# Grouped-query attention and a gated feed-forward: where q and k are transposed, and where the spatial bias is added

## The chip, the core and the metric

The kernel runs on one core of one Trainium2 chip. The metric is the device time of one execution in microseconds. TensorE (PE in the profile, with PEld for its weight loads) does matmuls, VectorE is DVE, ScalarE is ACT, GpSimd is POOL, and SyncE (SP) issues most of the DMAs. [...]

## The reference

Eight batches of attention, 16 query heads on 4 key heads, 384 positions, head size 64; its output, rows of 1024, goes through a feed-forward with a gate that mixes positions.

```python
scores = scale * np.matmul(q, k.transpose(0, 1, 3, 2))
scores = scores - np.max(scores, axis=-1, keepdims=True)
attn = np.exp(scores)
attn = attn / (np.sum(attn, axis=-1, keepdims=True) + 1e-09)
x = np.matmul(attn, v)                      # per head, then heads side by side
h = np.maximum(x @ w_in, 0.0)
u, v = (h[..., :d_ff // 2].copy(), h[..., d_ff // 2:].copy())
v_n = (v - mu) / np.sqrt(var + 1e-06)       # mu, var over the last axis
v_s = np.einsum('ts,bsd->btd', w_spatial, v_n) + b_spatial[None, :, None]
gated = u * v_s
return (gated @ w_out).astype(np.float32)
```

All inputs and the output are fp32; the matmuls take fp16. `w_spatial` is 384 x 384, `b_spatial` has 384 entries.

## The kernel before

A batch is worked in nine visits (`vi` 0 to 8, the loop at line 457). A visit issues two of the 18 score units of its batch (`scores`, L268: two matmuls of 512 columns into a two-bank PSUM tile `sc`, of which there are two; then one ScalarE exponential, L281, into `aT`). Four times a batch, at the visits of `VALUES_AT`, comes `values`: the sums of the exponentials (`sums`), their reciprocal on ScalarE (`rec`, a logarithm and an exponential), and two products with v (`X`), which VectorE multiplies by `rec` into `xT` (L312).

The feed-forward of batch b-1 runs between the visits of batch b, from a queue of 17 pieces: three `mk_v` (`pv`, relu on ScalarE, statistics and normalisation on VectorE into `v_n`), four `mk_u` (`pu`, relu on VectorE into `uT`, L371), four `mk_sp` (`psp`, the spatial product of one 128-wide slice m of the features, gated into `gT`, L389), six `mk_out` (`po`, L403, which contracts over all four slices of `gT`; VectorE copies it out, L410, and SP stores it). Each piece has a planned cost; per visit, pieces are taken until the spent cost passes a budget (`per_visit`, line 454). The last feed-forward runs alone at the end.

PE, POOL and SP follow the order in which the program issues their instructions; the order on VectorE and ScalarE is left to the scheduler. Eight PSUM banks are in use: four for the two score tiles, and four that all other products share in turn (the pool `ps`).

At visit 2 of batch b, `load_batch` (line 134) loads k, q and v of batch b+1 in fp32 and casts them to fp16: on POOL, but for k and the first half of q of batch 1, which VectorE casts. q and k have to be transposed before the scores. Batch 0 does so on PE (`transpose_k`, `transpose_q`: six 128 x 128 transposes into a PSUM tile `pk` or `pq`, then one VectorE copy of 768 fp16 a partition, L244 and L258). Batches 1 to 7 do so by DMA from SBUF to SBUF, issued on SP (`dma_transpose_k`, `dma_transpose_q`, L221 and L228): k and the first half of q (`gp` 0) at visit 6 of the batch before, the second half at visit 8.

The spatial bias is one number per output position, that is per column of `psp`. It is added by a first matmul (L380) of a matrix of ones rows with `bias_rows`, which holds the bias as two fp16 rows, a high and a low part. `load_bias` makes them once (L172 to L174), from a 1.5 KB load.

On POOL, the weights of the feed-forward are loaded in the opening by 34 DMAs with a cast from fp32 (L188, L194), in its queue ahead of the casts of v and of the second half of q of batch 1.

Of the kernel before, what the change touches and what calls it, by code (L numbers as in the profile page):

```python
# [10 lines left out]
FP32 = mybir.dt.float32  # L11
FP16 = mybir.dt.float16
# [6 lines left out]
def kernel(  # L19
# [92 lines left out]
    def cast_k(b, engine):  # L112
        k16 = qk16.tile([P, NGP, NST, 2, D], FP16, name=f"k16_{b}", tag="k16")
        k32 = loaded["k32", b].rearrange("p (gp h) (t d) -> p gp t h d", gp=NGP, t=NST)
        for gp in range(NGP):
            engine.tensor_copy(k16[:, gp], k32[:, gp])  # L116
        loaded["k16", b] = k16
# [6 lines left out]
    def cast_q(b, gp, engine):  # L124
        q16 = qk16.tile([P, G, NST, 2, D], FP16, name=f"q16_{b}_{gp}", tag=f"q16_{gp}")
        q32 = loaded["q32", b, gp]
        for half in range(2):
            engine.tensor_copy(
                q16[:, :, :, half, :],
                q32[:, half * G : (half + 1) * G, :].rearrange("p j (t d) -> p j t d", t=NST),  # L130
            )
# [17 lines left out]
    bias_rows = cst.tile([P, S], FP16, name="bias_rows")  # L149
    bias_ones = cst.tile([P, P], FP16, name="bias_ones")  # L150
# [4 lines left out]
    def load_consts():  # L155
# [4 lines left out]
        nc.vector.memset(bias_rows, 0.0)  # L160
        nc.vector.memset(bias_ones, 0.0)
        nc.vector.memset(bias_ones[0:1, :], 1.0)
        nc.vector.memset(bias_ones[32:33, :], 1.0)

    def load_bias():
        b32 = cst.tile([1, S], FP32, name="b32")
        lo32 = cst.tile([1, NST, P], FP32, name="lo32")
        nc.sync.dma_start(b32, moe_b_spatial.rearrange("(a s) -> a s", a=1))
        b_tp = b32.rearrange("a (p t) -> a t p", t=NST)
        hi = bias_rows[0:1, :].rearrange("a (t p) -> a t p", t=NST)  # L170
        lo = bias_rows[32:33, :].rearrange("a (t p) -> a t p", t=NST)
        nc.vector.tensor_copy(hi, b_tp)  # L172
        nc.vector.tensor_tensor(lo32, b_tp, hi, ALU.subtract)
        nc.vector.tensor_copy(lo, lo32)  # L174
# [44 lines left out]
    def dma_transpose_k(b):  # L219
        kT[b] = tr_sb.tile([P, NGP, NST, P], FP16, name=f"kT_{b}", tag="kT")  # L220
        nc.sync.dma_start_transpose(  # L221
            kT[b].rearrange("p g t q -> p (g t) q"),
            loaded["k16", b].rearrange("p g t h d -> p (g t h d)"),
        )

    def dma_transpose_q(b, gp):
# [295 lines left out]
```

## Time and profile before

| | us |
|---|---|
| median of 3 runs (lowest to highest) | 290.18 (289.11 to 290.86) |
| the profiled execution | 289.11 |
| its span, first to last instruction | 287.3 |
| start of pv_0, batches 0 to 7 of the feed-forward | 41.1, 74.6, 106.7, 138.6, 170.4, 202.9, 235.3, 264.1 |

Each step of the last row but the first and the last is one batch. The profile by stretches of about one batch, with the busy time of each engine and the mean granted clock of PE:

```profile
75.00:107.00 32.00, 30.44 (x278) 13.34 (x276) 16.61 (x31) 22.73 (x32) 4.92 (x7) 1.00 0.65 153
107.00:139.00 32.00, 30.58 (x278) 13.46 (x277) 16.14 (x31) 23.03 (x33) 4.93 (x7) 1.00 0.66 156
...
235.00:267.00 32.00, 31.80 (x280) 14.45 (x280) 16.58 (x32) 19.59 (x28) 0.00 (x0) 1.00 0.16 65
```

The columns are the stretch, its length, the busy time and instruction count of PE, PEld, DVE, ACT and POOL, the clock, the mean busy share of the DMA engines and the GB/s. A matmul's duration in the profile reaches past the start of the next one[...]; the distance between two starts is what a matmul costs. An idle stretch of an engine is shown in square brackets behind the instruction that ended it, with what released it.

### The profile page before, as it was taken

Reading aid. Unit: us, or ns where it says so; the run is one execution under the profiler, and the core shown is the slowest. Engines: PE = TensorE matmul, PEld = TensorE weight load, DVE = VectorE, ACT = ScalarE, POOL = GpSimd, SP = SyncE. Lnnn points to the kernel's source line nnn. Section 1 sums busy time; section 2 is a strip of 40 time slices with the busy share of each in tenths; the row PEclk is TensorE's granted clock in tenths of the full one; section 3 lists DMA queues with packets and bytes.
Section 4 is the critical chain, followed back from the end, with each engine's and each line's share of the span. In section 5 each row is a group of like instructions: output and inputs, shape, how many; then the busy total and the mean of one; then the engine's idle time right before and its main releaser. Section 6 shows DMA issues by size and latency. Waiting matters only on the chain.

```text
span 287.3 us, 5420 instructions
## 1 busy us (share of the span) xinstructions
PE 255.2 (89%) x2247; PEld 113.3 (39%) x2247; DVE 143.8 (50%) x277; ACT 184.4 (64%) x249; POOL 54.0 (19%) x88
## 2 busy tenths in 40 slices
PE   0685879989899989999899989999899989999993
PEld 0431234444344334444344434443344434444551
DVE  3427116474365443574365434674365434575673
ACT  1485895757676686758676776658676786664300
POOL 0654870600140004200150003300150000000000
PEclk9998599999999999999999999999999999999998
DMA  7999999906691479709790549406790530003105
GB/s 215 331 252 124 147 142 216 287 20 198 203 260 29 112 157 312 108 0 203 227 248 13 130 160 329 70 2 202 241 245 2 128 148 0 2 29 121 73 0 219
DMA packets 59402, 42.42 MB, mean 148 GB/s; under 512 B 29041, under 2 KB 55666, under 8 KB 59378
## 3 DMA queue, kind: packets, MB, share of 16 engines
q1 hardware_dynamic: 56274, 38.94, 53.6%
q0 software_dynamic: 3104, 3.15, 7.9%
q8 instruction: 17, 0.28, 0.4%
q14 instruction: 7, 0.06, 0.1%
HBM read 25.76 MB, written 12.58 MB: 133 GB/s over the span
## 4 chain that ended last, share of the span: by engine, by line
PE 75%; ACT 11%; DMA 6%; DVE 4%; issue 1%; SPq 1%; POOL 0%
DMA ws_318<-in_moe_w_spatial_dram 4%; DMA q_0_1_136<-in_q_dram 3%; ACT aT_1_337 L281 1%; ACT aT_0_2652 L281 1%; ACT aT_0_2216 L281 1%; ACT aT_0_471 L281 1%; ACT aT_0_1780 L281 1%; ACT aT_0_1344 L281 1%; ACT aT_0_3088 L281 1%; ACT aT_0_908 L281 1%; ACT aT_1_3288 L281 1%; ACT aT_1_686 L281 1%; SPq L106 1%; DVE ws_320 L204 1%; PE pv_0_3166 L327 1%
## 5 line engine op out<-in xcount | busy, mean ns | idle before, releaser
L364 PEld LDWEIGHTS <-w_in_107 128*128 128x128 f16 x256 | 23.4, 98 | 22.8 <-issue 8.8
L188 POOL DMA_DIRECT2D w_in_107<-in_moe_w_in_dram x32 | 17.2, 544 | 8.1 <-DMA w_in_107<-in_moe_w_in_dram 8.1
L296 PEld LDWEIGHTS <-ones_103 128*32 128x32 f16 x384 | 7.4, 97 | 15.8 <-issue 14.1
L238 PE MATMUL pk_178<-ident_102,k_0_128 128*128 128x128 f16 x6 | 0.8, 303 | 8.4 <-DVE ident_102 L157 8.4
L281 ACT ACTIVATE aT_0_210<-sc_0_204 128x1024 f16<-128x1024 f32 x1 | 1.0, 1023 | 9.1 <-PE sc_0_204 L268 9.1
L268 PEld LDWEIGHTS <-kT_185 64*128 64x128 f16 x36 | 2.1, 103 | 10.9 <-issue 10.8
L116 POOL CAST k_5_1861<-k_5_1857 128x384 f16<-128x384 f32 x2 | 1.0, 507 | 24.3 <-DMA k_5_1857<-in_k_dram 24.3
L116 POOL CAST k_6_2297<-k_6_2293 128x384 f16<-128x384 f32 x2 | 1.0, 507 | 24.1 <-DMA k_6_2293<-in_k_dram 24.1
L116 POOL CAST k_4_1425<-k_4_1421 128x384 f16<-128x384 f32 x2 | 1.0, 508 | 23.5 <-DMA k_4_1421<-in_k_dram 23.5
L116 POOL CAST k_7_2733<-k_7_2729 128x384 f16<-128x384 f32 x2 | 1.0, 508 | 23.4 <-DMA k_7_2729<-in_k_dram 23.4
L296 PEld LDWEIGHTS <-v_0_139 128*32 128x32 f16 x96 | 3.2, 122 | 5.0 <-issue 4.2
L116 POOL CAST k_3_989<-k_3_985 128x384 f16<-128x384 f32 x2 | 1.0, 507 | 20.6 <-DVE mv_1004 L338 20.6
L380 PEld LDWEIGHTS <-bias_ones 128*128 128x128 f16 x32 | 3.1, 97 | 4.3 <-issue 2.7
L204 DVE CAST ws_320<-ws_318 128x384 f16<-128x384 f32 x3 | 1.9, 672 | 5.7 <-DMA ws_318<-in_moe_w_spatial_dram 5.7
L238 PEld LDWEIGHTS <-k_0_128 128*128 128x128 f16 x6 | 0.6, 133 | 8.3 <-DVE k_0_128 L116 4.6
L312 DVE TENSOR_TENSOR xt_273<-X_1_0_0_435,rec_1_0_432 128x384 f16<-128x384 f32 x1 | 0.6, 558 | 6.5 <-ACT rec_1_0_432 L308 6.5
L327 PEld LDWEIGHTS <-xt_3225 128*128 128x128 f16 x24 | 2.4, 98 | 2.8
L403 PEld LDWEIGHTS <-gT_3644 128*128 128x128 f16 x24 | 2.3, 98 | 3.0 <-DVE gT_3644 L389 0.5
L327 PEld LDWEIGHTS <-xt_624 128*128 128x128 f16 x24 | 2.3, 98 | 2.8 <-issue 0.2
L327 PEld LDWEIGHTS <-xt_2808 128*128 128x128 f16 x24 | 2.3, 98 | 2.8 <-issue 0.2
L327 PEld LDWEIGHTS <-xt_2372 128*128 128x128 f16 x24 | 2.3, 98 | 2.8 <-issue 0.2
L327 PEld LDWEIGHTS <-xt_273 128*128 128x128 f16 x24 | 2.3, 98 | 2.8 <-issue 0.2
(1077 smaller groups left out, 755.9 us busy)
## 6 DMA issues: line engine op xcount, KB each, us to landing
w_in_107<-in_moe_w_in_dram POOLq DMA_DIRECT2D x32, 64.0 KB, 5.4
w_out_108<-in_moe_w_out_dram POOLq DMA_DIRECT2D x2, 512.0 KB, 7.8
q_0_0_125<-in_q_dram SPq DMA_DIRECT2D x2, 384.0 KB, 4.9
q_0_1_136<-in_q_dram SPq DMA_DIRECT2D x2, 384.0 KB, 7.5
q_1_0_248<-in_q_dram SPq DMA_DIRECT2D x1, 768.0 KB, 6.6
q_1_1_258<-in_q_dram SPq DMA_DIRECT2D x1, 768.0 KB, 8.5
q_2_0_536<-in_q_dram SPq DMA_DIRECT2D x1, 768.0 KB, 7.7
q_2_1_546<-in_q_dram SPq DMA_DIRECT2D x1, 768.0 KB, 7.8
```

The costliest lines, as they stand in the source:

```text
L106: nc.sync.dma_start(q32[:, i * n : (i + 1) * n, :], q[b, h0 : h0 + n].rearrange("h (p t) d -> p h (t d)", t=NST),)
L116: engine.tensor_copy(k16[:, gp], k32[:, gp])
L188: nc.gpsimd.dma_start(w_in16[32 * i : 32 * (i + 1), kc : kc + 2, c0:c1], rows[jq])
L204: nc.vector.tensor_copy(ws16[:, tt, :, :], ws32[:, tt, :].rearrange("p (s t) -> p t s", t=NST))
L238: nc.tensor.transpose(pk[:, gp, t, :], k16[:, gp, t, :, :].rearrange("p h d -> p (h d)"), ident16,)
L268: nc.tensor.matmul(sc[:, half, :], kT[b][lo:hi, gp, t, :], rhs[lo:hi, c * 512 : (c + 1) * 512], start=True, stop=True,)
L281: nc.scalar.activation(aT[b, gp][:, t, :, c * 512 : (c + 1) * 512], sc, AF.Exp, scale=scale)
L296: nc.tensor.matmul(dst[32 * i : 32 * (i + 1), 0:S], weights(t, half), a[:, t, half, j * S : (j + 1) * S], start=(t == 0), stop=(t == NST - 1),
L327: nc.tensor.matmul(pv, xt[:, kc, st * P : (st + 1) * P], w_in16[:, kc, DH:DFF], start=(kc == 0), stop=(kc == NKT - 1),)
L364: nc.tensor.matmul(pu[:, 0:S], w_in16[:, kc, mu * P : (mu + 1) * P], xT[b][:, kc, :], start=(kc == 0), stop=(kc == NKT - 1),)
L380: nc.tensor.matmul(psp[:, 0:S], bias_ones, bias_rows, start=True, stop=False)
L403: nc.tensor.matmul(po, gT[:, m, tt * P : (tt + 1) * P], w_out16[:, m, half * 512 : (half + 1) * 512], start=(m == 0), stop=(m == NDT - 1),)
```

## The change

q and k of every batch are transposed on PE. The DMA transposes and their functions go, and `k16` and `q16` are laid out with the tile index t in front. `transpose_k` of the next batch is issued at visit 6, `transpose_q` of its first half at visits 7 and 8, and of the second half at visits 1 and 2 of its own batch; each counts 0.36 in the planned cost.

The bias matmul goes. `bias_b` holds the bias in fp32 on all 128 partitions, loaded once by a broadcasting DMA. VectorE adds it to `psp` while it moves it to SBUF (`v_s`, fp32, three buffers); the product with `uT` is a second operation, on GpSimd for the feed-forwards of batches 0 to 6 and on VectorE for the last. The planned cost of a spatial piece goes from 0.66 to 0.50. In the order that follows from the new costs, po_0_0 comes straight behind psp_3, and score units 14 and 15 behind it.

```diff
     def cast_k(b, engine):
-        k16 = qk16.tile([P, NGP, NST, 2, D], FP16, name=f"k16_{b}", tag="k16")
-        k32 = loaded["k32", b].rearrange("p (gp h) (t d) -> p gp t h d", gp=NGP, t=NST)
-        for gp in range(NGP):
-            engine.tensor_copy(k16[:, gp], k32[:, gp])
+        k16 = qk16.tile([P, NST, HKV, D], FP16, name=f"k16_{b}", tag="k16")
+        engine.tensor_copy(k16, loaded["k32", b].rearrange("p g (t d) -> p t g d", t=NST))
...
     def cast_q(b, gp, engine):
-        q16 = qk16.tile([P, G, NST, 2, D], FP16, name=f"q16_{b}_{gp}", tag=f"q16_{gp}")
+        q16 = qk16.tile([P, NST, G, 2, D], FP16, name=f"q16_{b}_{gp}", tag=f"q16_{gp}")
...
-                q32[:, half * G : (half + 1) * G, :].rearrange("p j (t d) -> p j t d", t=NST),
+                q32[:, half * G : (half + 1) * G, :].rearrange("p j (t d) -> p t j d", t=NST),
...
-    bias_rows = cst.tile([P, S], FP16, name="bias_rows")
-    bias_ones = cst.tile([P, P], FP16, name="bias_ones")
+    bias_b = cst.tile([P, S], FP32, name="bias_b")
...
     def load_bias():
-        b32 = cst.tile([1, S], FP32, name="b32")
-        lo32 = cst.tile([1, NST, P], FP32, name="lo32")
-        nc.sync.dma_start(b32, moe_b_spatial.rearrange("(a s) -> a s", a=1))
-        b_tp = b32.rearrange("a (p t) -> a t p", t=NST)
-        hi = bias_rows[0:1, :].rearrange("a (t p) -> a t p", t=NST)
-        lo = bias_rows[32:33, :].rearrange("a (t p) -> a t p", t=NST)
-        nc.vector.tensor_copy(hi, b_tp)
-        nc.vector.tensor_tensor(lo32, b_tp, hi, ALU.subtract)
-        nc.vector.tensor_copy(lo, lo32)
+        nc.sync.dma_start(bias_b, moe_b_spatial.partition_broadcast(P))
...
             psp = ps.tile([P, 512], FP32, name=f"psp_{b}_{m}", tag="ps")
-            nc.tensor.matmul(psp[:, 0:S], bias_ones, bias_rows, start=True, stop=False)
             for st in range(NST):
                 nc.tensor.matmul(
                     psp[:, 0:S],
                     held["v_n", b, st][:, m * P : (m + 1) * P],
                     wsT16[:, st, :],
-                    start=False,
+                    start=(st == 0),
                     stop=(st == NST - 1),
                 )
+            v_s = moe_sb.tile([P, S], FP32, name=f"v_s_{b}_{m}", tag="v_s", bufs=3)
             nc.vector.tensor_tensor(
-                held["gT", b][:, m, :], psp[:, 0:S], held["uT", b][:, m, :], ALU.mult
-            )
+                v_s.rearrange("p (t s) -> p t s", t=NST),
+                psp[:, 0:S].rearrange("p (t s) -> p t s", t=NST),
+                bias_b.rearrange("p (s t) -> p t s", t=NST),
+                ALU.add,
+            )
+            gate = nc.gpsimd if b < B - 1 else nc.vector
+            gate.tensor_tensor(held["gT", b][:, m, :], v_s, held["uT", b][:, m, :], ALU.mult)
...
-            + [(0.66, mk_sp(b, m)) for m in range(NDT)]
+            + [(0.50, mk_sp(b, m)) for m in range(NDT)]
...
-    T_VALUES = 1.55
+    T_SCORE, T_VALUES, T_TRANS = 0.62, 1.55, 0.36
...
-        per_visit = (total + 4 * T_VALUES) / VISITS
+        per_visit = (total + 4 * T_VALUES + 5 * T_TRANS) / VISITS
...
-                    if b == 0 and vi in (1, 2):
+                    if vi in (1, 2):
                         transpose_q(b, 1, vi - 1)
+                        done += T_TRANS
                     if vi == 2 and b + 1 < B:
                         load_batch(b + 1, nc.vector if b == 0 else nc.gpsimd)
-                    if vi == 6 and b + 1 < B:
-                        dma_transpose_k(b + 1)
-                        dma_transpose_q(b + 1, 0)
-                    if vi == 8 and b + 1 < B:
-                        dma_transpose_q(b + 1, 1)
+                    if vi >= 6 and b + 1 < B:
+                        if vi == 6:
+                            transpose_k(b + 1)
+                        else:
+                            transpose_q(b + 1, 0, vi - 7)
+                        done += T_TRANS
```

`transpose_k`, `transpose_q` and their callers otherwise stay; they only index the new layouts.

## The prediction

> **What bounds the kernel now.** I read the page first (busy shares, chain of waits), then PE's timeline of one batch, then the other engines' timelines of the same stretch, then the opening and the last microseconds. The times below are those of the profiled execution (289.1 us, of which 287.3 are span).
>
> ```profile
> PE 255.2 (89%) x2247; PEld 113.3 (39%) x2247; DVE 143.8 (50%) x277; ACT 184.4 (64%) x249; POOL 54.0 (19%) x88
> ...
> PE 75%; ACT 11%; DMA 6%; DVE 4%; issue 1%; SPq 1%; POOL 0%
> ```
>
> PE carries the chain, and the chain's 6% of DMA are two loads in the opening (ws, q_0_1); no transposing DMA is on it. A batch takes 31.8 us: pv_0 starts at 138.6 and again at 170.4. PE's timeline there:
>
> ```profile
> 154.36 0.38 PE L268 MATMUL sc_13_2086<-qT_1_1765,kT_1655 64*128 64x512 f16 x2
> 154.68 0.34 PE L380 MATMUL psp_0_2096<-bias_rows,bias_ones 128*128 128x384 f16 x1
> 154.85 0.33 PE L382 MATMUL psp_0_2096<-wsT_109,v_n_0_1922 128*128 128x384 f16 x1
> ...
> 157.12 0.33 PE L382 MATMUL psp_3_2114<-wsT_109,v_n_2_1926 128*128 128x384 f16 x1
> 157.38 0.39 PE L268 MATMUL sc_14_2120<-qT_1_1765,kT_1655 64*128 64x512 f16 x2
> 157.61 0.38 PE L268 MATMUL sc_15_2123<-qT_1_1765,kT_1655 64*128 64x512 f16 x2
> 157.92 1.04 PE L403 MATMUL po_0_0_2129<-w_out_108,gT_2095 128*128 128x512 f16 x4
> ...
> 169.15 0.39 PE L268 MATMUL sc_4_2285<-qT_0_2093,kT_2091 64*128 64x512 f16 x2 [0.90 <-ACT aT_0_2216 L281]
> 170.07 0.39 PE L268 MATMUL sc_5_2288<-qT_0_2093,kT_2091 64*128 64x512 f16 x2 [0.52 <-ACT aT_0_2216 L281]
> ```
>
> The starts are what to read: PE runs on without a gap but for 0.90 + 0.52 us before sc_4 and sc_5, where four score units in a row wait for two score buffers. So PE work that is added outside those gaps costs its full length, and so does a wait in PE's hand-written order. DVE in the same stretch:
>
> ```profile
> 154.90 0.55 DVE L371 TENSOR_SCALAR uT_1981<-pu_3_2073 128x384 f16<-128x384 f32 x1
> 155.54 0.56 DVE L389 TENSOR_TENSOR gT_2095<-psp_0_2096,uT_1981 128x384 f16<-128x384 f32 x1
> ...
> 157.49 0.56 DVE L389 TENSOR_TENSOR gT_2095<-psp_3_2114,uT_1981 128x384 f16<-128x384 f32 x1
> ```
>
> The gate of each psp is one DVE operation; the last ends at 158.05. po_0_0 needs all four, in turn, and sc_14 and sc_15 cover the last one.
>
> [...] No two-input operation runs on POOL in this trace; its casts (507 ns for 384, 827 ns for 768) give 0.83 ns an element and about 187 ns fixed. [...] The trace shows half clock from about 26.2 to 36.4[...] and what set it off was a window only one third busy[...]:
>
> ```profile
> 22.74:26.15 3.41, 1.15 (x26) 0.63 (x25) 3.38 (x7) 2.36 (x4) 2.63 (x5) 1.00 1.36 181
> 26.15:29.56 3.41, 2.60 (x18) 0.70 (x18) 1.90 (x5) 1.56 (x2) 1.15 (x3) 0.50 1.33 100
> ```
>
> (columns: PE, PEld, DVE, ACT, POOL busy, granted clock, DMA share, GB/s).
>
> **The change part by part.** The order of instructions of the changed kernel gives what stands where.
>
> *Bias matmul gone:* four of 0.163 us (spacing of the psp starts), so -0.65 us a batch.
>
> *Transposes on PE:* 30 a batch, in five groups of six: pk and two pq in vi 6 to 8, two pq in vi 1 and 2. The warm transposes of L213 (57.38 and 57.55 for three) are 0.057 us apart: 0.34 us a group. pq_1_0 stands between sc_3 and sc_4, in the 0.90 us gap: free, while ACT sets that gap. Four groups are exposed, 1.37 us. A new operand shape costs PE 0.11 us (pu 1.41 after scores, 1.30 after another pu), but the groups take that step over from a neighbour. If the weight load (98 ns) set the pace instead, 24 x 0.041 = 1 us a batch more. I take 0.057, it is measured.
>
> *PSUM to SBUF copies:* five of 0.557 us on DVE, 2.8 us a batch on an engine half idle. One matters: the copy of pk stands between uT 3 and the first bias add.
>
> *Bias add on DVE, gate on POOL:* each psp now passes two engines, and in the new order po_0_0 follows psp_3 at once, with sc_14 and sc_15 behind it. On the clock of the batch above: pk ends 154.74+0.11+0.34 = 155.19, psp_0 155.68, psp_3 157.15. DVE: uT 3 until 155.37, copy of pk until 155.85, then the adds. An add reads the bias with a stride of three floats; nearest row L173, a tensor_tensor on 384 strided fp32, 654 ns (unstrided 556): I take 0.65, one every 0.57. First gate at 156.6. A POOL gate: [...] estimate 0.93, one every 0.90; bounds 0.55 (the adds' pace is then the limit) and 1.2. Fourth gate done at 156.6 + 3 x 0.90 + 0.93 = 160.23. po_0_0's last matmul waits for it, ends 160.52, then the scores (0.54), then pq_0_0 (0.45): po_0_1 starts at 161.5 in place of 158.96, +2.55. Bias matmul, pk and pq_0_0 are in that. With pq_0_1 and pq_1_1 (0.34 each) a batch gains **3.23 us**. Behind po_0_0 wait sc_14, sc_15 and ACT's exponentials; ACT has over 8 us of slack a batch, so nothing follows. Casts on POOL's queue ahead of the gates end at 150.0, 6 us earlier.
>
> Six batches (b = 1 to 6) at 3.23 = 19.4. In b = 7 there is no pk and no pq of a next batch: first gate at 156.1, po_0_0 done 160.05, +1.65. Middle: **+21.0**.
>
> *Tail:* for the last batch both operations are DVE's: eight in a row, add, add, gate, gate twice. From 275.25: four adds at 0.57 and four gates at 0.47 and the last's end make 279.9, against 277.86 for the last gate now: **+2.0**.
>
> *Opening:* now DVE stands behind the ws cast until ws lands:
>
> ```profile
> 12.56 10.06 DMA ws_318<-in_moe_w_spatial_dram
> 22.64 1.86 DVE ws_320 L204 x3
> 24.49 0.57 DVE bias_rows L172
> ```
>
> Three bias operations (0.64, 0.65, 0.35) in front of and among the xt products disappear; the DMA transposes of batch 1 leave the DMA engines, which in 14.4 to 21.5 moved 252 GB/s after 331 in the slice before: 24% of 7 us, so ws lands about 1.7 us earlier. Together 3.0 to 3.3 us at X_0_1_1, which now waits 2.38. New wait: PE's pq_1_0 of batch 1 stands ahead of sc_4 and needs q_1_1, cast on POOL behind 34 weight loads:
>
> ```profile
> 37.34 1.45 POOL L194 DMA_DIRECT2D w_out_108<-in_moe_w_out_dram  x2
> 38.78 0.84 POOL L121 CAST v_1_260<-v_1_256 128x768 f16<-128x768 f32 x1
> 39.55 1.60 POOL L128 CAST q_1_1_262<-q_1_1_258 128x768 f16<-128x768 f32 x2
> ```
>
> It is cast at 41.15, when pv_0 now starts. Of POOL's 8.1 us of waits for weight loads about 5 fall after 20 us, when the transposes take most DMA time; without them the cast is done near 36, PE arrives near 35 and pv_0 starts about 38.5. I take **-2.5** (bounds +2, if POOL gains nothing, and -6.6: ACT alone, 22 exponentials at 0.92 and three pairs at 1.05 from 11.1, reaches 34.5). The broadcast load of the bias has until 60 us.
>
> *Clock:* over the 3.2 us of the stall PE does four matmuls; a window that lies full on it is a quarter busy, like the one that set off the half clock. Estimate one of seven stalls: a window at half clock, **+1.7** (bounds 0 and 7 x 1.7 = 11.9).
>
> Sum: 21.0 + 2.0 - 2.5 + 1.7 = +22.2: 311.3 from the profiled 289.1. The median of the runs is 1.1 higher (290.18), so I name 312.
>
> **Rivals.**
> 1. *Gates nearly hidden.* At 0.55 us a gate the adds set the pace: fourth gate at 158.86, a batch 1.83, b = 7 +0.3, tail +2, opening -2.5: +10.8, 301. [...]
> 2. *The clock falls at every stall,* or the gate takes 1.2 us (4 x 0.27 x 7 = 7.6): 311.3 + 10.2 = 321.5, or 311.3 + 7.6 = 318.9. For it: the one-third-busy window[...].
> 3. *Not slower: the opening.* Its place is 12 to 41 us, its most 6.6. It decides only if the middle and tail together cost less than that, which needs hidden gates and 1.37 us of transposes in shadow too: 6 x 0.46 + 0.3 + 2.0 - 6.6 = -1.5, 288.6. Against: PE's starts leave no shadow but the 1.4 us.
>
> **How the numbers follow.** The forecast's mechanism (304 to 318) 0.68; rival 1 0.12; rival 2 0.16; rival 3 0.04, of which half within 0.5%, about what a measurement here can tell from no change. Faster 0.02, same 0.02, slower 0.96. Range 301 to 322: gates from 0.55 to 1.2 us and the clock's bounds; outside it some 2 in 10.
>
> **What would show it.** Right: a gap of PE of 2 to 3 us over po_0_0, released by POOL gates; POOL gate near 0.93; a batch near 35 us; pv_0 of batch 0 near 38.5. Wrong: no wait at po_0_0, or gates faster than the adds; transposes far from 57 ns; half clock in most batches; pv_0 after 41.

## The result and the profile after

| | before | after |
|---|---|---|
| median (lowest to highest), us | 289.64 (288.39 to 290.86), 4 runs | 322.64 (317.95 to 324.48), 4 runs |
| after / before, 95% interval | | 1.1045 [1.0901, 1.1189] |
| the profiled execution, us | 289.11 | 323.44 |
| mean granted clock in it | 0.979 | 0.957 |
| a batch in which the clock stays full, us | 31.82 | 35.40 |

The runs of the changed kernel lie 2% apart, and the ratio, here and in the table of the experiments, is taken from a kernel's quicker runs alone (two of the four here), while the median is of all and the profile is of one of the slower two, with a mean clock of 0.957 where the quicker two have 0.972. The change costs 33 us by the medians, about 30 by the ratio. The forecast was 312, its range ended at 322.

The page of the changed kernel, busy times, the clock row and the chain of waits by engine:

```profile
PE 276.2 (86%) x2425; PEld 124.8 (39%) x2425; DVE 163.0 (51%) x307; ACT 184.5 (57%) x249; POOL 77.9 (24%) x110
...
PEclk9997879999999899979999999979999799999989
...
PE 55%; ACT 15%; POOL 11%; DMA 7%; DVE 7%; issue 2%; SPq 1%; POOLq 0%
```

The clock row of the kernel before:

```profile
PEclk9998599999999999999999999999999999999998
```

PE's share of the chain of waits goes from 75% to 55%, POOL's from nothing to 11% (some 24 us of these 35 are the gates, most of the rest is POOL's work in the opening). The clock row, a digit for each 8 us, has 7s and 8s in the middle of the span that the kernel before does not have.

PE's timeline in the middle of the batch whose clock stays full (155.2 to 190.6), from the transposes of k to the queries behind po_0_0:

```profile
171.29 0.51 PE L209 MATMUL pk_2235<-ident_102,k_5_2006 128*128 128x128 f16 x6
171.64 0.33 PE L352 MATMUL psp_0_2245<-wsT_108,v_n_0_2066 128*128 128x384 f16 x1
...
173.43 0.33 PE L352 MATMUL psp_3_2266<-wsT_108,v_n_2_2070 128*128 128x384 f16 x1
174.16 0.39 PE L379 MATMUL po_0_0_2274<-w_out_107,gT_2244 128*128 128x512 f16 x1 [0.41 <-POOL gT_2244 L367]
175.03 0.39 PE L379 MATMUL po_0_0_2274<-w_out_107,gT_2244 128*128 128x512 f16 x1 [0.48 <-POOL gT_2244 L367]
...
176.77 0.39 PE L379 MATMUL po_0_0_2274<-w_out_107,gT_2244 128*128 128x512 f16 x1 [0.48 <-POOL gT_2244 L367]
177.09 0.39 PE L239 MATMUL sc_14_2280<-qT_1_1977,kT_1766 64*128 64x512 f16 x2
```

The starts tell the cost: the six transposes take 0.35 us (171.29 to 171.64). The four matmuls of po_0_0 start 0.87 us apart, where po_0_1 behind them, with its gates ready, takes 0.87 for all four. From the last psp_3 matmul (173.43) to sc_14 (177.09) PE spends 3.66 us, of which about 1.2 is the pace of its own five matmuls: a wait of some 2.4 us, though the brackets add up to 1.85, since the records are longer than the steps: a psp_3 matmul is recorded with 0.33 us and the next starts 0.16 behind it. What sets the pace is on POOL and DVE. First POOL, then DVE, same stretch:

```profile
173.19 0.92 POOL L367 TENSOR_TENSOR gT_2244<-v_s_0_2249,uT_2125 128x384 f16<-128x384 f32 x1 [6.59 <-DVE v_s_0_2249 L360]
174.06 0.92 POOL L367 TENSOR_TENSOR gT_2244<-v_s_1_2256,uT_2125 128x384 f16<-128x384 f32 x1
```

```profile
172.44 0.66 DVE L360 TENSOR_TENSOR v_s_0_2249<-psp_0_2245,bias_b 128x384 f32<-128x384 f32 x1
173.03 0.66 DVE L360 TENSOR_TENSOR v_s_1_2256<-psp_1_2252,bias_b 128x384 f32<-128x384 f32 x1
```

A gate is 0.92 us, one each 0.87, slower than the adds (one each 0.58), so POOL falls behind from the second slice on and PE takes over its step of 0.87.

**The clock.** Stretches of half clock begin at 28.0, 41.7, 103.1, 140.7, 212.4, 249.9 and 311.3. From the first to the last it is 283.3 us, 83 times 3.413, and the distances between them are 4.01, 17.99, 11.02, 21.01, 10.99 and 17.99 times that: all lie on one raster. The stretch from 103.1 ends one such step later, at 106.5, and that from 28.0 two steps later, at 34.9. The table below is cut on that raster, in pairs: the window that lies on a batch's stall, and the one after it (columns as in the stretches of the kernel before; the third last number is the clock).

```profile
99.71:103.12 3.41, 1.63 (x6) 0.50 (x8) 1.04 (x3) 0.00 (x0) 2.89 (x4) 1.00 0.00 0
103.12:106.54 3.42, 3.42 (x15) 1.37 (x12) 1.35 (x3) 1.94 (x2) 0.00 (x0) 0.50 0.00 0
137.25:140.66 3.41, 1.97 (x10) 0.52 (x10) 1.06 (x2) 0.22 (x1) 2.38 (x3) 1.00 0.00 0
140.66:144.08 3.42, 3.42 (x14) 1.50 (x13) 1.40 (x3) 1.72 (x2) 0.00 (x0) 0.50 0.00 0
174.80:178.21 3.41, 2.22 (x15) 0.87 (x16) 0.77 (x3) 0.69 (x1) 1.91 (x3) 1.00 0.00 0
178.21:181.62 3.41, 3.41 (x28) 1.39 (x30) 2.59 (x4) 1.78 (x3) 0.00 (x0) 1.00 0.30 121
...
284.03:287.44 3.41, 2.14 (x10) 0.67 (x11) 0.82 (x2) 0.61 (x1) 1.99 (x3) 1.00 0.00 0
287.44:290.86 3.42, 3.42 (x35) 1.41 (x37) 2.07 (x3) 2.12 (x3) 0.00 (x0) 1.00 0.38 151
```

The stall is the same in every batch; where the raster cuts it differs. With 1.62 to 1.97 us of recorded PE time in the window (the two pairs left out have 1.79 and 1.62), the next window runs at 0.50; with 2.14 or 2.22 it runs at full clock, and so it does behind the stall of the first batch, with about 2.25. Such a window, at a granted clock of 0.50, costs half of its length, 1.71 us, and the batches that hold the four falls in the middle (37.04, 37.08, 37.26, 37.03) are longer than the 35.40 one by about that (1.63 to 1.86).

**The account,** from the two profiled executions (+34.3 us):

| part | forecast | measured | how |
|---|---|---|---|
| seven batches in the middle, without the clock | +21.0 | +21.6 | distances of the pv_0 starts (from pv_1 for the first), less 1.7 for each fall |
| tail | +2.0 | +1.6 | end minus last pv_0: 26.45 less 23.18, less one fall of 1.7 |
| opening | -2.5 | +2.7 | pv_1 at 45.53 against 42.84 |
| clock in the stalls | +1.7 | +8.5 | four falls in the middle, one in the tail |
| sum | +22.2 | +34.4 | |

### The profile page after: what moved, and what is told of

It reads as the page before. It is cut to its first block, busy times and chain, and to the rows that moved or that the text cites. A ratio compares the mean times of both kernels' runs of the same rounds, so it can differ in the third digit from the quotient of the medians.

```text
span 321.7 us, 5797 instructions
## 1 busy us (share of the span) xinstructions
PE 276.2 (86%) x2425; PEld 124.8 (39%) x2425; DVE 163.0 (51%) x307; ACT 184.5 (57%) x249; POOL 77.9 (24%) x110
## 4 chain that ended last, share of the span: by engine, by line
PE 55%; ACT 15%; POOL 11%; DMA 7%; DVE 7%; issue 2%; SPq 1%; POOLq 0%
DMA w_in_106<-in_moe_w_in_dram 5%; DMA q_0_1_130<-in_q_dram 3%; POOL w_in_106 L173 3%; ACT aT_1_3095 L252 1%; ACT aT_1_2619 L252 1%; ACT aT_1_2143 L252 1%; ACT aT_1_1667 L252 1%; ACT aT_1_1191 L252 1%; ACT aT_1_710 L252 1%; ACT aT_0_2391 L252 1%; POOL gT_1292 L367 1%; POOL gT_3196 L367 1%; POOL gT_2244 L367 1%; POOL gT_1768 L367 1%; POOL gT_816 L367 1%
## 5 line engine op out<-in xcount | busy, mean ns | idle before, releaser
L335 PEld LDWEIGHTS <-w_in_106 128*128 128x128 f16 x256 | 23.4, 98 | 21.7 <-issue 7.6
L367 POOL TENSOR_TENSOR gT_3645<-v_s_0_3650,uT_3535 128x384 f16<-128x384 f32 x1 | 0.9, 914 | 33.1 <-DVE v_s_0_3650 L360 33.1
L252 ACT ACTIVATE aT_0_204<-sc_0_198 128x1024 f16<-128x1024 f32 x1 | 1.0, 1024 | 10.5 <-PE sc_0_198 L239 10.5
L114 POOL CAST k_5_2006<-k_5_2002 128x768 f16<-128x768 f32 x1 | 0.8, 822 | 19.4 <-DMA k_5_2002<-in_k_dram 19.4
L114 POOL CAST k_4_1530<-k_4_1526 128x768 f16<-128x768 f32 x1 | 0.8, 822 | 18.9 <-DMA k_4_1526<-in_k_dram 18.9
L114 POOL CAST k_7_2958<-k_7_2954 128x768 f16<-128x768 f32 x1 | 0.8, 822 | 18.9 <-DMA k_7_2954<-in_k_dram 18.9
L379 PEld LDWEIGHTS <-gT_3913 128*128 128x128 f16 x24 | 2.7, 114 | 6.6 <-DVE gT_3913 L367 3.1
L379 PEld LDWEIGHTS <-gT_1768 128*128 128x128 f16 x24 | 2.7, 116 | 6.5 <-POOL gT_1768 L367 3.1
L114 POOL CAST k_6_2482<-k_6_2478 128x768 f16<-128x768 f32 x1 | 0.8, 822 | 17.3 <-DMA k_6_2478<-in_k_dram 17.3
L114 POOL CAST k_3_1054<-k_3_1050 128x768 f16<-128x768 f32 x1 | 0.8, 823 | 17.3 <-DMA k_3_1050<-in_k_dram 17.3
L379 PEld LDWEIGHTS <-gT_1292 128*128 128x128 f16 x24 | 2.5, 110 | 6.2 <-POOL gT_1292 L367 3.1
L379 PEld LDWEIGHTS <-gT_3196 128*128 128x128 f16 x24 | 2.5, 109 | 6.2 <-POOL gT_3196 L367 3.1
L379 PEld LDWEIGHTS <-gT_2720 128*128 128x128 f16 x24 | 2.4, 105 | 5.8 <-POOL gT_2720 L367 3.1
L209 PEld LDWEIGHTS <-k_0_123 128*128 128x128 f16 x6 | 0.6, 133 | 9.7 <-DVE k_0_123 L114 5.1
L379 PEld LDWEIGHTS <-gT_3645 128*128 128x128 f16 x24 | 2.2, 97 | 5.7 <-POOL gT_3645 L367 3.1
L379 PEld LDWEIGHTS <-gT_2244 128*128 128x128 f16 x24 | 2.2, 97 | 5.4 <-POOL gT_2244 L367 3.1
```

The source lines that it names most:

```text
L114: engine.tensor_copy(k16, loaded["k32", b].rearrange("p g (t d) -> p t g d", t=NST))
L209: nc.tensor.transpose(pk[:, gp, t, :], k16[:, t, 2 * gp : 2 * gp + 2, :].rearrange("p g d -> p (g d)"), ident16,)
L252: nc.scalar.activation(aT[b, gp][:, t, :, c * 512 : (c + 1) * 512], sc, AF.Exp, scale=scale)
L335: nc.tensor.matmul(pu[:, 0:S], w_in16[:, kc, mu * P : (mu + 1) * P], xT[b][:, kc, :], start=(kc == 0), stop=(kc == NKT - 1),)
L367: gate.tensor_tensor(held["gT", b][:, m, :], v_s, held["uT", b][:, m, :], ALU.mult)
L379: nc.tensor.matmul(po, gT[:, m, tt * P : (tt + 1) * P], w_out16[:, m, half * 512 : (half + 1) * 512], start=(m == 0), stop=(m == NDT - 1),)
```

## The experiments

Theory: a batch pays for PE's wait over po_0_0, the transposes' own length, and a half-clock window wherever the raster lies on the wait; the opening is set by POOL's cast of q_1_1. Rivals: the gate's engine is what costs; the clock falls for another reason than the wait; the wait only moves elsewhere when it is covered. In the table below, "us" is the median of all runs and the ratio is to the kernel before on the same chip. The other columns are of one profiled execution: "batch" is one whose clock stays full, "falls" are the half-clock windows that begin between pv_1 of batch 0 and the last pv_0, and "pv_0" is the start of the first one.

| kernel | us | ratio [95%] | batch | falls | pv_0 |
|---|---|---|---|---|---|
| the changed kernel | 322.64 | 1.1045 [1.0901, 1.1189] | 35.40 | 4 | 42.5 |
| e1_transposes_only | 301.86 | 1.0424 [1.0358, 1.0490] | 33.68 | 0 | 41.1 |
| e2_bias_only | 298.51 | 1.0315 [1.0245, 1.0386] | 33.04 | 0 | 38.9 |
| e3_gate_vector | 321.97 | 1.1105 [1.1029, 1.1181] | 35.40 | 5 | 41.5 |
| e4_fill | 316.11 | 1.0925 [1.0857, 1.0994] | 35.40 | 0 | 42.7 |
| e5_casts_vector | 318.91 | 1.1022 [1.0949, 1.1095] | 35.41 | 4 | 39.3 |
| e7_spread | 320.53 | 1.1070 [1.0991, 1.1150] | 36.52 | 3 | 42.1 |
| e11_spread_unpaired | 313.22 | 1.0870 [1.0810, 1.0931] | 35.44 | 0 | 42.0 |
| e12_fill_casts | 313.23 | 1.0835 [1.0772, 1.0898] | 35.41 | 0 | 38.3 |
| e13_cover | 309.13 | 1.0687 [1.0645, 1.0730] | 34.43 | 0 | 42.8 |
| e8_best | 303.38 | 1.0480 [1.0414, 1.0546] | 33.08 | 5 | 37.9 |
| e9_ws_late | 291.44 | 0.9975 [0.9946, 1.0005] | 31.83 | 1 | 37.4 |
| e10_ws_pool | 287.03 | 0.9929 [0.9902, 0.9956] | 31.83 | 0 | 37.8 |

### The two halves of the change

e1_transposes_only is the changed kernel with the bias as the kernel before adds it, and its gate:

```diff
             psp = ps.tile([P, 512], FP32, name=f"psp_{b}_{m}", tag="ps")
+            nc.tensor.matmul(psp[:, 0:S], bias_ones, bias_rows, start=True, stop=False)
...
-            v_s = moe_sb.tile([P, S], FP32, name=f"v_s_{b}_{m}", tag="v_s", bufs=3)
             nc.vector.tensor_tensor(
...
+                held["gT", b][:, m, :], psp[:, 0:S], held["uT", b][:, m, :], ALU.mult
+            )
```

> The changed kernel with the bias as before: bias matmul on PE, one VectorE operation that gates psp. Transposes stay on PE, and PE's order stays that of the changed kernel. My theory (the gate chain is the larger part): four exposed groups of six transposes, +1.37 us a batch, and the opening of the changed kernel (pv_1 of the first feed-forward 2.7 us later than before), no fall of the clock at po_0_0: about 301 us (298 to 305), a batch near 33.3 us, the fourth gate done about 0.6 us after psp_3. Rival (the transposes and their VectorE copies are the larger part of the loss, by filling VectorE and holding the PSUM buffers): 310 us or more, a batch of 35 us or more.

e2_bias_only is the kernel before with the changed kernel's bias add, gate and planned cost, and its DMA transposes kept:

```diff
-            nc.tensor.matmul(psp[:, 0:S], bias_ones, bias_rows, start=True, stop=False)
...
+            v_s = moe_sb.tile([P, S], FP32, name=f"v_s_{b}_{m}", tag="v_s", bufs=3)
             nc.vector.tensor_tensor(
-                held["gT", b][:, m, :], psp[:, 0:S], held["uT", b][:, m, :], ALU.mult
-            )
...
+            gate = nc.gpsimd if b < B - 1 else nc.vector
+            gate.tensor_tensor(held["gT", b][:, m, :], v_s, held["uT", b][:, m, :], ALU.mult)
...
-            + [(0.66, mk_sp(b, m)) for m in range(NDT)]
+            + [(0.50, mk_sp(b, m)) for m in range(NDT)]
```

> The kernel before with only the bias part of the change: fp32 add on VectorE, gate on GpSimd, no bias matmul; transposes by DMA as before, and score units 14 and 15 stand between psp_3 and po_0_0. My theory: po_0_1 starts 0.9 us later a batch (fourth gate 2.3 us after the last score unit), 6.6 us over seven batches, +2 us in the tail, -1 in the opening, at most two falls of the clock (1.7 each): about 299 us (295 to 303). Rival (the bias part alone makes up the loss): 310 us or more. If both this and the transposes-only kernel stay near 300, what is missing to 320 is the order (score units 14 and 15 behind po_0_0) and the clock.

The transposes alone make a batch 1.86 us longer (forecast 1.37 for the four exposed groups), the bias and gate alone 1.22. Together they make 3.08 of the 3.58 that the changed kernel shows; the other half microsecond is only there when both are. Neither alone has a fall in the middle, so the 6.8 us of clock belong to the combination too: by the ratios the halves cost 4.2% and 3.2%, the whole 10.5%. Part of the combination is the order. In e2_bias_only the score units 14 and 15 still stand between psp_3 and po_0_0; in e1_transposes_only they stand behind po_0_0, as in the change, but its gates are there in time and PE does not wait for them. Only with both halves do the slow gates meet that order; e13_cover below takes the order back. The opening splits in the same way. With the bias change alone pv_0 starts 2.2 us earlier than before, with the transposes alone where it did (41.14), with both 1.4 us later.

### Is it the gate's engine?

```diff
-            gate = nc.gpsimd if b < B - 1 else nc.vector
+            gate = nc.vector
```

> The changed kernel with the gate on VectorE in all batches, nothing on GpSimd but the casts. My theory (what costs is two operations in a row behind each psp, wherever they run): VectorE needs 4 x 0.57 + 4 x 0.47 for its eight, so the fourth gate ends at the same moment as with GpSimd's four of 0.91: 318 to 324 us, no change outside the spread of the changed kernel. Rival (GpSimd's slower operation is the cost): the wait over po_0_0 shrinks by 1.5 us or more a batch, 305 to 311 us.

The batch is 35.40, as with the gate on POOL, and the clock falls in five stalls. PE now waits twice over po_0_0 (1.7 us in all, the longer 1.2) for a DVE that does eight operations in a row, four adds of one each 0.58 and four gates. That is as long as one add and four gates on POOL. The ratios, 1.1105 and 1.1045, lie within each other's intervals. So the price of the gate on POOL is no reason by itself: two passes over each slice, in front of a consumer that needs all four at once, cost it on either engine.

### Is it the wait or the clock?

e4_fill gives PE twelve matmuls of no use ahead of po_0_0; their result is never read.

```diff
         def f():
+            if b < B - 1 and tt == 0 and half == 0:
+                fill = ps.tile([P, 512], FP32, name=f"fill_{b}", tag="ps")
+                for i in range(12):
+                    nc.tensor.matmul(
+                        fill[:, 0:S], ident16, wsT16[:, i % NST, :], start=(i == 0), stop=(i == 11)
+                    )
             if half == 0:
```

> The changed kernel with twelve matmuls of 384 columns more, into a PSUM tile that nobody reads, between psp_3 and po_0_0 of the seven batches with a GpSimd gate: 1.96 us of PE work more a batch inside a wait of 2.4 us. My theory (the wait leaves a window of PE thin and halves the clock for 3.4 us, at 1.7 us a time): no fall of the clock at po_0_0 any more, mean clock 0.98 or more, 312 to 317 us, faster than the changed kernel although it does more. Rival (the falls of the clock have another cause, or cost nothing): mean clock as before, 320 us or more.

PE's timeline of e4_fill where the stall was (in the traces of the experiments the names carry no numbers):

```profile
171.38 2.11 PE L376 MATMUL fill<-wsT,ident 128*128 128x384 f16 x12
173.33 0.81 PE L385 MATMUL po<-w_out,gT 128*128 128x512 f16 x3
174.56 0.39 PE L385 MATMUL po<-w_out,gT 128*128 128x512 f16 x1 [0.42 <-POOL gT L367]
174.88 0.61 PE L239 MATMUL sc<-qT,kT 64*128 64x512 f16 x4
```

The useless work takes 1.95 us (171.38 to 173.33) and only the last gate is still waited for. Batches 2 to 6 take 35.40 to 35.74, so filling it makes no batch shorter than the full-clock one of the changed kernel, but no window falls to half clock between 46 and 312. The kernel with twelve matmuls more a batch is faster by 6.5 us by the medians; by the ratios it is 1.2%, and the intervals of the two overlap. The firmer comparison is with e3, run on the same chip at the same time, with a batch of the same 35.40 us and the wait unfilled: it is 5.9 us above e4, the intervals lie apart, and its mean clock is 0.960 to 0.971 in its four runs, where e4's is 0.981 to 0.988. This separates the two terms: the wait itself costs what it did, and the falls come from the wait, for they go when PE is kept busy in it.

### The opening

```diff
-        cast_v(b, nc.gpsimd)
-        cast_q(b, 1, nc.gpsimd)
+        cast_v(b, first)
+        cast_q(b, 1, first)
```

> The changed kernel with the casts of v and of the second half of q of batch 1 on VectorE, as the other casts of batch 1 are. My theory (in the opening PE waits 2.6 us in its order for a cast that stands on GpSimd's queue behind the 34 weight loads, and the clock falls there): the wait before pq_1_0 of batch 1 is gone, pv_1 of the first feed-forward starts near 42 in place of 45.5, 316 us (313 to 319). Rival (the opening is set by the loads themselves, which are slower because batch 2 is now loaded at 15 us): pv_1 stays at 45 or later, PE waits for weights or ws in place of the cast, 319 us or more.

`first` is VectorE for batch 1, so the casts of v_1 and q_1_1 no longer stand behind POOL's weight loads. pv_0 starts at 39.3, 3.2 us earlier than in the changed kernel, pq_1_0 waits for nothing, and the clock stays full in the opening. The median is 3.7 us lower, but the two ratios, 1.1022 and 1.1045, do not tell the kernels apart: the earlier start is shown by the trace, not by the total. The middle is untouched, with four falls in the profiled execution.

How the opening came to be set by that cast, the chain of waits of the changed kernel shows:

```profile
36.98 1.46 POOL w_out_107 L179 x2
38.43 0.84 POOL v_1_253 L119
39.27 1.54 POOL q_1_1_255 L126 x2
```

and PE's timeline, how the wait of 2.62 us is followed by a pv_0 of 3.17 us, most of it at half clock (from 41.7), where it takes 1.90 in the kernel before:

```profile
40.85 0.51 PE L224 MATMUL pq_1_0_535<-ident_102,q_1_1_255 128*128 128x128 f16 x6 [2.62 <-POOL q_1_1_255 L126]
...
42.53 3.17 PE L298 MATMUL pv_0_578<-w_in_106,xt_266 128*128 128x512 f16 x8
```

SP's queue tells why the DMA engines did not become free. First before, then after:

```profile
14.12 1.73 SPq L221 DMA_TRANSPOSE kT_399<-k_1_250  x1
15.92 7.84 SPq L228 DMA_TRANSPOSE qT_0_401<-q_1_0_253  x1
41.17 2.50 SPq L228 DMA_TRANSPOSE qT_1_463<-q_1_1_262  x1
43.72 0.74 SPq L93 DMA_DIRECT2D k_2_534<-in_k_dram  x1
```

```profile
15.28 0.39 SPq L93 DMA_DIRECT2D k_2_559<-in_k_dram  x1
17.68 0.38 SPq L106 DMA_DIRECT2D q_2_0_561<-in_q_dram  x1
```

The transposes held up SP's queue until q_1_1 was cast (SP's wait for that cast is 17.3 us), and with it the loads of batch 2. Without them k_2 and q_2_0 (1.2 MB) are issued 28 us earlier, between the weight loads. The core moves 223 GB/s in the first 45 us, 200 before. That these loads take what the transposes left is read from the queue; it was not tried by holding them back.

### Moving the wait

e7_spread takes the pieces in the order u0, u1, u2, sp0, sp1, u3, sp2, sp3, and both halves of an output in turn over the slices, so that each gate is followed by two matmuls.

```diff
-            + [(1.30, mk_u(b, mu)) for mu in range(NDT)]
-            + [(0.50, mk_sp(b, m)) for m in range(NDT)]
-            + [(0.87, mk_out(b, tt, h)) for tt in range(NST) for h in range(2)]
+            + [u[0], u[1], u[2], sp[0], sp[1], u[3], sp[2], sp[3]]
+            + [(1.74, mk_out(b, tt)) for tt in range(NST)]
...
             for m in range(NDT):
+                for half in range(2):
+                    nc.tensor.matmul(
+                        po[half],
```

> The changed kernel with its four spatial pieces spread (psp_0 and psp_1 ahead of pu_3, psp_2 and psp_3 behind) and the two halves of an output tile taken together, slice by slice, so that four matmuls run before the third gate is needed. The same operations in all. My theory (the loss in the middle is a wait in PE's order for a chain of fixed length, so work put beside the chain takes it away): the wait over po_0_0 falls from 2.4 to about 0.7 us, no fall of the clock there, 12 us for the waits and 5 for the clock: about 302 us (299 to 307). Rival (GpSimd and VectorE are short of throughput at that place): the wait moves to another instruction and 312 us or more remain.

PE's waits in e7_spread's full-clock batch (79.34 to 115.86): total us, times, longest.

```profile
PE sc L239 <- ACT aT L252: 1.5, 2, 1.0
PE po L380 <- DVE xt L283: 0.8, 1, 0.8
PE po L380 <- POOL gT L367: 0.7, 2, 0.5
PE pu L335 <- DVE xt L283: 0.5, 1, 0.5
```

The wait for the gates goes from 1.8 (by the same view) to 0.7 us, as wanted, and the batch gets longer, 36.52. Two new waits on DVE's xt operations, with which DVE empties shared PSUM banks, take 1.3 us, and the wait before sc_4 grows from 0.5 to 1.0. The clock's falls did not go either; they moved with the thinnest place to the score waits (they begin at 152.6, 190.1 and 227.7). The rival that the wait moves was right.

e11_spread_unpaired keeps that order of the pieces and the outputs single:

```diff
-            + [(1.74, mk_out(b, tt)) for tt in range(NST)]
+            + [(0.87, mk_out(b, tt, h)) for tt in range(NST) for h in range(2)]
```

(against e7_spread; `mk_out` is the changed kernel's.)

> The changed kernel with the spatial pieces spread over pu_3 as before, but the output pieces one half at a time, as in the change. Theory A (what took the gain of the spread kernel was taking the two output halves together: two PSUM buffers at once, 0.8 us before po_2_1, and 0.55 us more before sc_4): without the pairing those two waits go, the wait over po_0_0 is about 1.3 us, 0.5 us remain before pu_3, a batch without a fall of the clock near 34.7 us, about 312 us (308 to 315). Theory B (the spread itself is what costs, by holding PSUM buffers from psp_0 on): a batch of 35.4 us or more, 318 us or more.

The time came out where the more favourable side had it, the batch where the other had it. A batch is 35.44, no shorter than the changed kernel's, while the median is 9.4 us lower (1.7% by the ratios, whose intervals just overlap). The gain is clock: the waits are the same in sum, but lie in several places, and no window in the middle falls. Its waits in one batch:

```profile
PE po L379 <- POOL gT L367: 1.4, 2, 0.9
PE sc L239 <- ACT aT L252: 1.0, 2, 0.5
PE pu L335 <- DVE xt L283: 0.5, 1, 0.5
```

Against e7_spread, the wait of 0.8 us of po on DVE and half a microsecond of score waits are gone and the gates cost 0.7 more; the wait of pu on DVE stays. So the first two belong to the pairs, which hold two PSUM banks at once, and the third to the order of the pieces.

e13_cover changes planned costs alone, so that sc_14, sc_15 and pq_0_0 come between psp_3 and po_0_0, as the scores did before:

```diff
-            + [(0.50, mk_sp(b, m)) for m in range(NDT)]
-            + [(0.87, mk_out(b, tt, h)) for tt in range(NST) for h in range(2)]
+            + [(1.37 if m == NDT - 1 else 0.50, mk_sp(b, m)) for m in range(NDT)]
+            + [
+                (0.87 if tt or h else 0.0, mk_out(b, tt, h)) for tt in range(NST) for h in range(2)
+            ]
```

> The changed kernel with one thing moved in PE's order: score units 14 and 15 and pq_0_0 ahead of po_0_0, in the place where the kernel before has its score units. My theory (the chain of adds and gates has a fixed end, so work put ahead of the waiting instruction is free): 0.54 us of scores and 0.45 us of transposes a batch go into the wait, a batch without a fall of the clock takes 34.4 us in place of 35.4, and with the wait broken up at most one fall over po_0_0 remains: 309 us (306 to 312). Rival (as with the spread pieces, another buffer or engine takes the gain back): a batch of 35.2 us or more, 313 us or more.

PE's timeline of e13_cover over the same place:

```profile
165.72 2.11 PE L352 MATMUL psp<-wsT,v_n 128*128 128x384 f16 x12
167.77 0.61 PE L239 MATMUL sc<-qT,kT 64*128 64x512 f16 x4
168.31 0.51 PE L224 MATMUL pq<-ident,q 128*128 128x128 f16 x6
168.65 0.86 PE L379 MATMUL po<-w_out,gT 128*128 128x512 f16 x2
169.99 0.39 PE L379 MATMUL po<-w_out,gT 128*128 128x512 f16 x1 [0.48 <-POOL gT L367]
170.86 2.98 PE L379 MATMUL po<-w_out,gT 128*128 128x512 f16 x13 [0.48 <-POOL gT L367]
```

Work that had to be done anyway stands in the stall: 0.88 us of it (167.77 to 168.65). The batch is 34.43, shorter by 0.97, and no window in the middle falls. It is 13.5 us less than the changed kernel by the medians (3.6% by the ratios, whose intervals lie apart), for a few planned costs. Of the 13.8 us between the two profiled executions, five falls fewer are some 8.5.

### Both at once

e12_fill_casts is e4_fill with the casts of e5_casts_vector.

> The changed kernel with both the filling matmuls and the VectorE casts of batch 1. If the accounts are additive: of the filled kernel's 316 the fall of the clock from 39 to 46 goes (3.4 us at most) and the wait for the cast (2.6 us): 311 us (309 to 313), mean clock above 0.99, no fall before the last batch. If the falls only move to another place: 314 us or more.

In the profiled execution (310.21 us) the mean clock is 1.000 as the profile rounds it, and pv_0 starts at 38.3. This is the changed kernel with the forecast's opening and no fall in the stalls; the forecast without its clock term was 289.1 + 20.5 = 309.6. The other three executions have mean clocks of 0.988, 0.978 and 0.978 and take 312.57 to 314.24 us, so the median lies just above the range that was expected; where their clock fell was not recorded.

### A version that beats both

In the kernel before, three casts of ws stand in DVE's queue ahead of the xt product that PE waits for. e9_ws_late delays the loads and the casts (`load_ws`, `load_bias`) to a later visit:

```diff
-                    if b == 0 and vi == 3:
+                    if b == 0 and vi == 8:
                         load_ws()
                         load_bias()
```

> The kernel before with only the later load of w_spatial (visit 8 of batch 0). My theory: VectorE no longer stands behind ws, PE's wait of 2.4 us before X_0_1_1 goes, and with it perhaps the fall of the clock in the opening: 286 us (284 to 288), so that of the gain of the version before it about 3 us belong to the opening. Rival (the opening is bound by the exponentials): 288 to 290 us.

In the profiled execution (291.72 us) pv_0 starts 3.7 us earlier, but the batch that follows takes 39.78 us (33.51 before), and the gain is gone; the ratio is 0.9975, with 1 inside its interval. PE's timeline shows where most of it goes:

```profile
54.14 2.72 PE L364 MATMUL pu<-xt,w_in 128*128 128x384 f16 x8 [3.56 <-DVE xt L312]
```

DVE stands behind the late ws, and PE behind DVE; a half-clock window follows this wait at 54. The wait moved. e8_best is the kernel before with the bias of the change, e7's order and pairing, and this late load.

> Transposes by DMA as before, the bias by VectorE and the gate by GpSimd as in the change, the spread order of the last experiment, and w_spatial loaded at visit 8 of batch 0 in place of visit 3, so that no VectorE cast waits for it in the opening. My theory: 0.65 us of bias matmul a batch saved, at most 0.1 us of wait at po_0_0, opening 2 to 4 us shorter: 282 us (279 to 286), faster than the kernel before. Rival (the two-operation gate costs more than the matmul it saves, also when spread): 287 us or more.

It takes 303.38 us, 21 more than was expected. pv_0 comes at 37.9, but a first batch of 41.3 takes that back, as in e9_ws_late; the full-clock batch of 33.08 is no shorter than that of e2_bias_only (33.04), so the spread with pairs gains nothing here; and the clock falls five times.

e10_ws_pool leaves the loads of the kernel before where they are and moves only the casts, of ws and of the bias, to GpSimd, behind its weight loads:

```diff
-            nc.vector.tensor_copy(
+            nc.gpsimd.tensor_copy(
                 ws16[:, tt, :, :], ws32[:, tt, :].rearrange("p (s t) -> p t s", t=NST)
...
+                if b == 0 and vi == 8:
+                    cast_ws()
+                    cast_bias()
```

> The kernel before with the casts of w_spatial and of the bias on GpSimd, behind its cast of q_1_1, in place of VectorE; all loads where they were. My theory: VectorE no longer stands behind the load of ws, PE's wait of 2.4 us before X_0_1_1 goes and pv_0 of the first feed-forward starts near 37.5 in place of 41.1, as in the last experiment, but nothing waits for ws later: 286 us (284 to 288), a ratio near 0.988. Rival (the start of the second batch takes the gain back, since its weights or its q come no earlier): 288.5 to 290.

pv_0 starts at 37.8, 3.3 us earlier, and the wait of X_0_1_1 is gone. PE gives some of it back 13 us later, where it waits for the DMA transposes of q:

```profile
50.91 0.39 PE L276 MATMUL sc<-qT,kT 64*128 64x512 f16 x2 [0.91 <-DMA qT<-q]
```

The first batch becomes 36.28 (33.51 before); a half-clock window that begins at 38.7 lies in it too. What remains is 0.7% below the kernel before (interval 0.4% to 1.0%), less than was expected, and the fastest of all.

## Why the prediction was right in sign and short by 11 us

1. **Bias matmul, transposes, gates: right.** The mechanism is the one forecast: PE over po_0_0 in steps of a POOL gate. The gate took 0.92, one each 0.87 (0.93 and 0.90 taken), the add 0.66, one each 0.58 (0.65 and 0.57), the transposes 0.35 a group (0.34). The 0.93 was the author's estimate: the trace of the kernel before has no two-input operation on POOL that shows the price of a gate. A batch came to 3.58 in place of 3.23. PE's starts in the two full-clock batches, laid upon each other at pv_0 (138.56 and 155.19), show where. First before, then after:

```profile
158.79 1.03 PE L403 MATMUL po_0_1_2135<-w_out_108,gT_2095 128*128 128x512 f16 x4
```

```profile
177.97 1.03 PE L379 MATMUL po_0_1_2297<-w_out_107,gT_2244 128*128 128x512 f16 x4
```

po_0_1 comes 2.55 us later, the forecast's figure, in which two slips cancel: it took 158.96, where a record ends, for the start before, and its sum, 161.5, lies 0.16 behind the 161.34 of the trace on the same clock. pq_1_0 costs nothing, as was forecast, and pq_1_1 its 0.35. Between po_0_1 and sc_2, where 0.34 was forecast for pq_0_1, it is 0.68: the output pieces stand in another order there, and po_2_0 waits 0.18 for ACT's `rec`. The rest was not followed up, nor why e1_transposes_only has the transposes alone at 1.86 where 1.37 was taken.
2. **Tail: right,** +1.6 for +2.0, clock apart. The forecast's own terms, four adds and four gates from 275.25, end at 279.5 and not at 279.9; that is +1.6, and DVE's eight operations take 4.27 us in the trace (306.40 to 310.67).
3. **Rival 1 (gates nearly hidden): out.** POOL is slower than the adds, one gate each 0.87 us against one add each 0.58. That this did not decide, the gate on VectorE shows.
4. **The clock term: the mis-sized one, +1.7 forecast, +8.5 measured.** The step read "a window that lies full on it is a quarter busy", and so one of seven, an estimate of the author's. A window need not lie full on the stall: the windows of 99.7 and 137.3 have 1.63 and 1.97 us of recorded PE time, 48% and 58%, and half clock follows all the same. The stall of 3.7 us is longer than the raster's 3.41, so much of it nearly always lies in one window. In the profiled execution four of seven fell, and the tail's too. The kernel before held a warning that the forecast did not use: its three thinnest windows on the raster after the opening have 1.99 to 2.00 us and no fall follows, so it ran close to the edge. Rival 2 named this, at 0.16, and its 321.5 is 1.1 us from the median; that is partly luck, since four of seven stalls fell and not all, and the opening made up the rest. Filling the wait (e4_fill), spreading it (e11) and covering it (e13) each removed the falls in the middle.
5. **The opening: the step that failed, -2.5 forecast, +2.7 measured.** Three reasons were given for the gain. "ws lands about 1.7 us earlier": it landed at 24.3, later than the 22.64 of before, and X_0_1_1 still waits 2.1 us (2.38). "Without them the cast is done near 36": it was done at 40.81, 0.34 earlier than before. Both took the DMA time of the transposes as freed. The prediction asked what the transposes leave on the DMA engines and not what they held back on SP's queue; that this is why the loads came no earlier is read from the queues, not tried. The size of the loss is less sure than its sign. In e3_gate_vector, with the same loads, ws was cast from 22.70 on, the cast of q_1_1 was done at 39.14 and pv_0 started at 41.53; in no kernel that transposes on PE and leaves that cast on POOL behind the weights was it done before 38.7. About one microsecond is not the change's: the second part of q_0_0 was there at 8.67 instead of 7.63, and that load's landing scatters by as much from kernel to kernel (PE's first transpose starts between 8.3 and 10.1 in the runs above). Third, PE's arrival near 35: right, as e5_casts_vector shows, where pq_1_0 starts without a wait at 36.23 and pv_0 at 39.34. There the forecast's opening came true to within 0.8 us. Unforeseen was the cast of q on VectorE in its new layout:

```profile
L126 DVE CAST q_0_0_125<-q_0_0_120 x2: 952/952/953, 5.2 to 8.7; 128x768 f16<-128x768 f32 x2
```

952 ns (shortest, median, longest of two), 1.24 ns an element of a partition, where the kernel before took 560, or 0.73 an element, for as many of the same types; POOL takes 827 for either layout. The trace shows what the new layout costs on VectorE, not why.

The median lies 0.6 us above the range. With the two terms at their measured size in the profiled execution, 311.3 + 6.8 + 5.2 = 323.3, its 323.44 comes out.

## What to carry to other kernels

Here a wait of TensorE cost its length and then, where it left one window of the clock with 1.58 to 1.97 us of recorded PE time in 3.41 (the changed kernel and e3_gate_vector), about 1.7 us more. A stall like the one here, 3.7 us in which PE waits 2.4, had a fall in four or five of seven occurrences in three kernels (the changed one, e3_gate_vector, e5_casts_vector); price it so, and put work that has to be done anyway into it, by the order of issue, before touching the engines that cause it. When a transfer is removed, ask what stood behind it in its queue: what can now start earlier may take the freed time. And when a change has two halves, price them together as well: here each alone had no fall of the clock in the middle, and both had four.

## What the runs showed of the hardware that was not expected

- In the profiled executions of the changed kernel and of e3_gate_vector half clock comes in windows of 3.413 us on one raster: in the first from 28.0 to 311.3, 83 windows apart, and in the second the falls begin at 66.5, 138.2, 175.7, 213.3 and 285.0, 21.01, 10.99, 11.02 and 21.01 windows apart. Where the stalls lie on the raster was seen in one execution of each only, so it was not shown that this is why the same kernel differs by 2% between executions; two runs of the changed kernel with the same mean clock, 0.972, lie 3.9 us apart (317.95 and 321.84).
- The windows ahead of these falls were not idle. In the changed kernel's stalls the edge lies between 1.97 and 2.14 us of recorded PE time in 3.41; in e3_gate_vector windows with 2.03 go either way (half clock behind the one from 63.1, full clock behind the one from 247.4). The recorded time alone does not tell: in the opening of the changed kernel windows with 1.15 us (from 7.6), as thin as the one in the prediction, and 1.87 us (from 21.2) are followed by full clock, one with 1.40 us (from 24.6) by half.
- Useless matmuls made the kernel faster: with twelve in each of seven batches e4_fill takes 5.9 us less than e3_gate_vector, whose full-clock batch is as long.
- A pair of output tiles that needs two of the four shared PSUM banks at once cost more here than it saved: with pairs (e7_spread) the waits for DVE and for the score buffers are 1.3 us longer than without (e11_spread_unpaired), those for the gates 0.7 shorter, and the batch is 1.08 us longer.
